# Attention products of blocks 2 to 8 as quarter-array matmuls

## The chip, the cores and the metric

The kernel runs on one core of a Trainium2 chip. The metric is the device time of one execution in microseconds (us), from the first to the last instruction of the core.

## What is computed

Attention within chunks of 64 tokens, for 8 batches, 8 heads, 576 tokens and a head width of 64; the 512 numbers that the heads leave for each of the 4608 tokens then go through a gated feed-forward layer of width 1536. All of it is float32.

```python
scores = scale * np.matmul(q_c, k_c.transpose(0, 1, 2, 4, 3))     # per chunk: 64 x 64 by 64
scores = scores - np.max(scores, axis=-1, keepdims=True)
attn = np.exp(scores)
attn = attn / (np.sum(attn, axis=-1, keepdims=True) + 1e-09)
out = np.matmul(attn, v_c)                                        # per chunk: 64 x 64 by 64
...
gate = 1.0 / (1.0 + np.exp(-(x @ w_gate)))
val = x @ w_val
return (gate * val @ w_out).astype(np.float32)
```

## The kernel before

**Blocks and units.** The tokens are worked through in 9 blocks of 512 (`m` = 0 to 8). The attention of a block is 4 units: `units[j]` is (block, half of the block's tokens, half of the heads), so block `m` has the units `4m` to `4m+3`. A unit holds 16 chunk products, laid out so that two heads lie on the two halves of the 128 partitions (`i`), and two others on the two halves of the result's partitions.

**Scores and values.** `products(j)` (lines 163 to 175) multiplies a unit's queries `qt` by its keys in 8 float32 matmuls. Each takes all 128 rows of TensorE's array and 64 of its 128 columns, and has 128 moving columns. Only 64 rows belong to one head, so the keys `kbd` are stored block-diagonally: head `i`'s keys on its own 64 partitions and zeros on the other 64, in a tile `[128, 2, 2, 256]` whose zeros are written once at the start. `values(j)` (lines 224 to 250) does the same with the softmax weights `pbd`, which are block-diagonal too, against the values `vt`: 8 matmuls of 64 by 128. Both write one PSUM bank per unit (`sc`, `av`, out of a pool of two banks with the tag `psa`). Consecutive matmuls alternate between the left and the right half of the array's columns (`c` in the scores, `a` in the values).

**How blocks 2 to 8 are interleaved.** The units from 8 on go in pairs through the generator `flow()` (lines 503 to 549). For a pair it issues, in this order: the score matmuls of both units (item "S"), the loads of the next pair, the last 4 of the 16 transposes of the pair before, maximum and subtraction on VectorE for each unit, one exponential on ScalarE, then the value matmuls of the pair before (item "A"), then sums, reciprocal, normalization, and 12 of the pair's own 16 transposes. `spread()` makes these on VectorE as 32 by 32 stream transposes out of `pr` into `pbd`. The items are pulled by `tick` and `insert` between steps of the feed-forward layer: the program order on TensorE and VectorE is the order in which this code runs, and is fixed when the kernel is built. There are 14 pairs (units 8 to 35), so 14 "S" bursts and 14 "A" bursts, each of 16 matmuls.

**The rest of TensorE's work.** For blocks 1 and 2, `hidden` and `down` make the feed-forward layer with matmuls in a split form (L261 and L287). Blocks 3 to 8 go in three pairs of blocks through a product scheme with 7 instead of 8 sub-products (`product`, L421) and the outward product (L496). These are 128 by 128 by 512 matmuls on `F32R` data, whose halves of higher and lower bits are made by ScalarE and VectorE.

**Evacuation.** From block 3 on, one ScalarE copy per unit (L242) moves `av` to a tile `raw`; in block 2 a ScalarE cast (L249) and a VectorE subtraction (L250) make the two `F32R` parts.

**Loads.** SP's queue issues all loads: `qt` by one transfer per unit, `kbd` by two (L152, one per half of the partitions, because the zeros lie between), `vt` by one.

Of the kernel before, what the change touches and what calls it, by code (L numbers as in the profile page):

```python
# [8 lines left out]
F32 = mybir.dt.float32  # L9
F32R = mybir.dt.float32r  # L10
U32 = mybir.dt.uint32
AF = mybir.ActivationFunctionType
ALU = mybir.AluOpType
AX = mybir.AxisListType

P = 128
D = 64
NB = 9
TB = 512
# [20 lines left out]
VECTOR_TRANSPOSES = 8  # L40

FIRST_PAIR = 3


SHARES = {1: 2.5, 2: 2.8, "up": 1.05, "down": 1.3}
# [3 lines left out]
def chunk_attn_moe(ctx: ExitStack, tc: tile.TileContext, q, k, v, w, out):  # L49


    nc = tc.nc
# [3 lines left out]
    xp = ctx.enter_context(tc.tile_pool(name="xp", bufs=4))  # L56
# [5 lines left out]
    ps_a = ctx.enter_context(tc.tile_pool(name="ps_a", bufs=2, space=bass.MemoryType.PSUM))  # L62
# [9 lines left out]
    pbd2 = const.tile([P, 2, 8, 2, D], F32, name="pbd")  # L72
# [67 lines left out]
    units = [(m, h, u) for m in range(NB) for h in range(2) for u in range(2)]  # L140
    state, both = {}, {}
    xt, raw = {}, {}

    def load(j):
        m, h, u = units[j]
        g = 2 * m + h
        qt = ap2.tile([P, 2, 256], F32, name="qt")
        kb = kbd[j % 2]
        nc.sync.dma_start(qt, q[g, u].rearrange("p (a n) -> p a n", a=2))
        for i in range(2):  # L150
            s = slice(i * D, (i + 1) * D)
            nc.sync.dma_start(kb[s, :, i, :], k[g, u, s].rearrange("p (a n) -> p a n", a=2))  # L152
        state[j] = dict(qt=qt, kb=kb)

    def load_values(j):
        m, h, u = units[j]
        vt = ap2.tile([P, 2, 4, D], F32, name="vt")
        nc.sync.dma_start(vt, v[2 * m + h, u].rearrange("p (a c d) -> p a c d", a=2, c=4))
        state[j]["vt"] = vt
# [3 lines left out]
    def products(j):  # L163
        s = state[j]
        sc = ps_a.tile([P, 512], F32, tag="psa", name="sc")
        for a in range(2):
            for t in range(2):
                for c in ((0, 1), (1, 0))[a * t]:
                    n0 = (2 * t + c) * D
                    nc.tensor.matmul(  # L170
                        sc[c * D:(c + 1) * D, (2 * a + t) * P:(2 * a + t + 1) * P],
                        lhsT=s["qt"][:, a, n0:n0 + D], rhs=s["kb"][:, a, :, n0:n0 + D],
                        start=True, stop=True,
                    )
        return sc.rearrange("p (g k) -> p g k", k=D)
# [48 lines left out]
    def values(j):  # L224
        m, h, u = units[j]
        s = state.pop(j)
        pb = pbd[j % 2]
        av = ps_a.tile([P, 512], F32, tag="psa", name="av")
        for c in range(4):
            for a in ((0, 1), (1, 0))[c == 3]:  # L230
                nc.tensor.matmul(  # L231
                    av[a * D:(a + 1) * D, c * P:(c + 1) * P],
                    lhsT=s["vt"][:, a, c, :], rhs=pb[:, 4 * a + c, :, :],
                    start=True, stop=True,
                )
        avv = av.rearrange("p (c h q) -> p h c q", h=2, q=D)
        if m >= FIRST_PAIR:
            n, half = divmod(m - FIRST_PAIR, 2)
            if (n, u) not in raw:
                raw[n, u] = xp.tile([P, 2, 2, TB], F32, tag="x", name="raw")  # L240
            dst = raw[n, u][:, :, half, h * 256:(h + 1) * 256]
            nc.scalar.copy(dst.rearrange("p h (c q) -> p h c q", q=D), avv)  # L242
            return
        if h == 0:
            xt[m, u] = xp.tile([P, 2, 2, TB], F32R, tag="x", name="xt")
        x = xt[m, u]
        hi = x[:, 0, :, h * 256:(h + 1) * 256].rearrange("p h (c q) -> p h c q", q=D)
        lo = x[:, 1, :, h * 256:(h + 1) * 256].rearrange("p h (c q) -> p h c q", q=D)
        nc.scalar.copy(hi, avv)  # L249
        nc.vector.tensor_tensor(out=lo, in0=avv, in1=hi.bitcast(F32), op=ALU.subtract)  # L250


    def up(m, f, which, tok):
# [40 lines left out]
    def evacuate(m, t, last=False):  # L294
        rows = out[m * TB + t * P:m * TB + (t + 1) * P, :]
        if last:
            ob = wp.tile([P, DM], F32, tag=f"u{t}", name="ob")
        elif m < FIRST_PAIR - 1 or t < 2:
            ob = mp.tile([P, DM], F32, name="ob")
# [91 lines left out]
    def operands(n):  # L391


        low = None
        for i, (name, (u, b), less) in enumerate(MADE):
            at = raw[n, u][:, :, b]
            if less:
                (u0, b0), (u1, b1) = less
                yield 1.2
                nc.vector.tensor_tensor(out=at, in0=raw[n, u0][:, :, b0], in1=raw[n, u1][:, :, b1], op=ALU.subtract)  # L400
            t = wp.tile([P, 2, 2, TB], F32R, tag=f"u{i}", name="xc")
            nc.scalar.copy(t[:, 0], at)
            if low:
                yield from lower(*low)
            low = n, name, t, at
        yield "wait"
        yield from lower(*low)
# [95 lines left out]
    def flow():  # L503


        kept = None
        for j in range(8, 4 * NB + 2, 2):
            more = j < 4 * NB
            if more:
                yield "S"  # L510
                scv = [products(j), products(j + 1)]
                if j + 2 < 4 * NB:
                    load(j + 2), load(j + 3)
                if kept:
                    yield from spread(*kept, range(12, 16))
                pr = ap2.tile([P, 2, 8, D], F32, name="pr", bufs=1)
                for i in range(2):
                    yield 1.4
                    mx = sm.tile([P, 8], F32, name="mx")
                    nc.vector.reduce_max(out=mx, in_=scv[i], axis=AX.X)  # L520
                    nc.vector.tensor_tensor(
                        out=pr[:, i], in0=scv[i], in1=mx.unsqueeze(2).broadcast_to([P, 8, D]), op=ALU.subtract)
                pr = pr.rearrange("p u g k -> p (u g) k")
                nc.scalar.activation(pr, pr, AF.Exp, scale=0.125)
            elif kept:
                yield from spread(*kept, range(12, 16))
            if kept:
                yield "A"
                values(j - 2), values(j - 1)
                if more:  # L530
                    load_values(j), load_values(j + 1)
            else:
                yield "wait"
            n, rest = divmod(j - 4 * FIRST_PAIR, 8)
            if n > 0 and rest == 0:
                yield ("open", n - 1)
                yield from operands(n - 1)
            if not more:
                return
            yield 1.5  # L540
            sums = sm.tile([P, 16], F32, name="sums2", bufs=1)
            nc.vector.reduce_sum(out=sums, in_=pr, axis=AX.X)
            nc.vector.tensor_scalar_add(out=sums, in0=sums, scalar1=1e-9)
            inv = sm.tile([P, 16], F32, name="inv2", bufs=1)
            nc.vector.reciprocal(out=inv, in_=sums)
            yield 1.2
            nc.vector.tensor_tensor(out=pr, in0=pr, in1=inv.unsqueeze(2).broadcast_to([P, 16, D]), op=ALU.mult)  # L547
            kept = pr, pbd2
            yield from spread(*kept, range(12))

    def spread(pr, pb, which):

        ps = pr.rearrange("p g (k j) -> p g k j", j=32)
        pb = pb.rearrange("p u (x c) h (i q) -> p (u x) c h i q", c=2, q=32)
        for n in which:
            c, i, h, k = n >> 3, n >> 2 & 1, n >> 1 & 1, n & 1
            src = slice((2 * c + i) * 32, (2 * c + i + 1) * 32)
            dst = slice((2 * h + k) * 32, (2 * h + k + 1) * 32)
            yield 0.44
            nc.vector.transpose(out=pb[dst, :, c, h, i, :], in_=ps[src, h::2, k, :])  # L560

    ahead = flow()
    now = dict(item=next(ahead), credit=0.0, ticks=0, since=0, unit=8, open=-1)

# [67 lines left out]
    kept = [(p, which, c) for p in range(6) for which in range(2) for c in range(2)]  # L632
# [9 lines left out]
    def rest():  # L642
        for m in range(1, FIRST_PAIR):
            upto = 4 * (m + 2) if m == 1 else 4 * (m + 3)
# [19 lines left out]
        for n in range(3):  # L664
            m0 = FIRST_PAIR + 2 * n
            upto = 4 * (m0 + 4)
# [77 lines left out]
```

## Time and profile before

| what | value |
|---|---|
| median of 3 runs | 955.29 us (955.13 to 955.56) |
| span of the profiled execution | 955.7 us (the profile shows nothing around it) |
| TensorE matmuls (PE) | 930.4 us, 97% of the span, 4960 records |
| VectorE (DVE) | 603.5 us, 63% |
| ScalarE (ACT) | 343.5 us, 36% |
| GpSimd (POOL) | 134.7 us, 14% |
| DMA, mean over 16 engines | 59.2% on the main queue |
| mean granted TensorE clock | 0.989 of full speed |

PE counts matmuls, PEld the loads of the stationary operand, which run beside matmuls. A busy share is time in which at least one instruction of the engine was under way. A float32 matmul of this kernel stands in the trace as two PE records and two PEld records (576 records each for the 288 score matmuls of 36 units); an `F32R` matmul as one of each. The "chain" is the work that ended last, followed back from the end of the span: what lies on it sets the time.

### The profile page before, as it was taken

The numbers are of one execution on the slowest core, as the hardware profiler recorded it, in microseconds if no ns is written. First come the engines' busy times: TensorE is split into PE (matmuls) and PEld (weight loads), VectorE is DVE, ScalarE is ACT, GpSimd is POOL, SyncE is SP. The second block draws the span as 40 slices with busy tenths as digits, with TensorE's granted clock in tenths as the row PEclk, the third lists the DMA queues.
The fourth block names the chain that finished last, engine by engine and source line by source line (L and its number), as shares of the span: only waits on it lengthen the run. The fifth ranks groups of instructions, "written<-read, shape, count | busy, mean of one in ns | idle before, by whom it ended". The sixth has DMA issues, their size and how long they took to land.

```text
span 955.7 us, 13079 instructions
## 1 busy us (share of the span) xinstructions
PE 930.4 (97%) x4960; PEld 764.1 (80%) x4960; DVE 603.5 (63%) x999; ACT 343.5 (36%) x558; POOL 134.7 (14%) x204
## 2 busy tenths in 40 slices
PE   5899999999999999999999999999999999999998
PEld 4777879888888887888887788888878888888886
DVE  5889875565676566867768575777586434545332
ACT  5889644232134343132242423213324321112222
POOL 1000004980049980000000000000000000000000
PEclk7899999999999999999999999999999999999999
DMA  8789886443233448666675756675555655556661
GB/s 262 215 292 306 285 293 198 133 133 88 67 123 121 133 149 292 198 210 200 213 238 218 242 199 213 208 230 200 197 198 205 206 206 188 198 187 209 220 220 45
DMA packets 81279, 189.61 MB, mean 198 GB/s; under 512 B 7488, under 2 KB 38208, under 8 KB 76608
## 3 DMA queue, kind: packets, MB, share of 16 engines
q1 hardware_dynamic: 81216, 188.77, 59.2%
q8 instruction: 39, 0.64, 0.3%
q14 instruction: 24, 0.20, 0.1%
HBM read 150.99 MB, written 37.75 MB: 197 GB/s over the span
## 4 chain that ended last, share of the span: by engine, by line
PE 88%; ACT 4%; DVE 4%; DMA 3%; issue 1%; SPq 0%; ACTq 0%; DVEq 0%
PE acc L496 20%; PE g L261 17%; PE cy L421 15%; PE cz L421 10%; PE cx L421 10%; PE acc L287 9%; PE sc L170 4%; PE av L231 3%; DMA w_raw<-w_in 2%; DMA kbd<-k_in 1%; ACT w_raw L129 1%; ACT w_raw L130 1%; ACT w L136 0%; DVE w L137 0%; ACT early L195 0%
## 5 line engine op out<-in xcount | busy, mean ns | idle before, releaser
L261 PE MATMUL g<-xt,w 128*128 128x512 f32 (+1 forms) x960 | 208.5, 372 | 9.5 <-ACT w L136 4.1
L261 PEld LDWEIGHTS g<-xt,w 128*128 128x128 f32 x960 | 168.4, 190 | 43.6 <-ACT w L136 4.3
L496 PE MATMUL acc<-wr,hh 128*128 128x512 f32 x576 | 177.8, 390 | 0.0
L421 PE MATMUL cy<-xc,wr 128*128 128x512 f32 x648 | 159.2, 389 | 0.9 <-DVE u L439 0.9
L421 PEld LDWEIGHTS cy<-xc,wr 128*128 128x128 f32 x648 | 121.5, 188 | 26.5 <-DVE u L439 1.3
L496 PEld LDWEIGHTS acc<-wr,hh 128*128 128x128 f32 x576 | 107.9, 188 | 22.7 <-ACT raw L242 0.3
L496 PE MATMUL acc<-wr,hl 128*128 128x512 f32 x288 | 112.7, 391 | 2.7 <-DVE hl L488 2.7
L421 PE MATMUL cz<-xc,wr 128*128 128x512 f32 x432 | 106.0, 391 | 0.0
L421 PE MATMUL cx<-xc,wr 128*128 128x512 f32 x432 | 106.0, 391 | 0.0
L560 DVE STREAM_TRANSPOSE pbd<-pr 32x256 f32<-32x256 f32 x224 | 97.7, 436 | 4.4 <-DVE pr L547 0.5
L488 DVE TENSOR_TENSOR hl<-hid,hh 128x512 fp32r<-128x512 f32 x72 | 49.4, 688 | 78.8 <-ACT hh L486 78.4
L421 PEld LDWEIGHTS cx<-xc,wr 128*128 128x128 f32 x432 | 80.6, 188 | 17.5 <-issue 1.0
L421 PEld LDWEIGHTS cz<-xc,wr 128*128 128x128 f32 x432 | 80.6, 188 | 17.5 <-issue 1.0
L287 PE MATMUL acc<-w,hh 128*128 128x512 f32 x288 | 91.3, 399 | 0.0
L486 ACT CAST hh<-hid 128x512 fp32r<-128x512 f32 x72 | 44.8, 622 | 127.1 <-PE acc L496 103.7
L496 PEld LDWEIGHTS acc<-wr,hl 128*128 128x128 f32 x288 | 54.0, 188 | 16.0 <-DVE hl L488 4.8
L338 POOL TENSOR_TENSOR a_val<-w 128x256 f32<-128x256 f32 x48 | 36.8, 787 | 211.6 <-DMA out<-ob 210.0
L439 DVE TENSOR_TENSOR u<-cy,s 128x512 f32<-128x512 f32 x36 | 24.8, 688 | 63.4 <-PE cy L421 63.1
L272 DVE TENSOR_TENSOR hf<-g,hf 128x512 f32<-128x512 f32 (+1 forms) x40 | 25.4, 635 | 60.9 <-PE g L261 60.3
L287 PEld LDWEIGHTS acc<-w,hh 128*128 128x128 f32 x288 | 53.2, 190 | 12.1 <-issue 1.9
L456 DVE TENSOR_TENSOR u<-cy,s 128x512 f32<-128x512 f32 x36 | 24.9, 691 | 50.9 <-PE cy L421 50.7
L287 PE MATMUL acc<-w,hl 128*128 128x512 f32 x144 | 56.5, 392 | 0.0
(103 smaller groups left out, 1013.8 us busy)
## 6 DMA issues: line engine op xcount, KB each, us to landing
wr<-sums SPq DMA_DIRECT2D x72, 512.0 KB, 4.6
wr<-outer SPq DMA_DIRECT2D x36, 1024.0 KB, 4.8
w_raw<-w_in SPq DMA_DIRECT2D x36, 512.0 KB, 5.3
wr<-given SPq DMA_DIRECT2D x36, 512.0 KB, 3.7
sums<-a_both SPq DMA_DIRECT2D x24, 512.0 KB, 3.5
qt<-q_in SPq DMA_DIRECT2D x36, 256.0 KB, 4.3
kbd<-k_in SPq DMA_DIRECT2D x72, 128.0 KB, 4.4
vt<-v_in SPq DMA_DIRECT2D x36, 256.0 KB, 3.9
```

The source lines that it names most:

```text
L170: nc.tensor.matmul(sc[c * D:(c + 1) * D, (2 * a + t) * P:(2 * a + t + 1) * P], lhsT=s["qt"][:, a, n0:n0 + D], rhs=s["kb"][:, a, :, n0:n0 + D],
L231: nc.tensor.matmul(av[a * D:(a + 1) * D, c * P:(c + 1) * P], lhsT=s["vt"][:, a, c, :], rhs=pb[:, 4 * a + c, :, :], start=True, stop=True,)
L261: nc.tensor.matmul(ps[:, tok], lhsT=wt[f, which][:, wpart, c:c + P], rhs=x[:, part, i, tok], start=n == 0, stop=n == 11)
L272: nc.vector.tensor_tensor(out=hf, in0=pv, in1=hf, op=ALU.mult)
L287: nc.tensor.matmul(acc[m, t], lhsT=hx[:, ts], rhs=wt[f, 2][:, wpart], start=f == 0 and i == 0, stop=f == NF - 1 and i == 2,)
L338: nc.gpsimd.tensor_tensor(out=val[:, 2 * n:2 * n + 2], in0=parts[:, 0], in1=parts[:, 1], op=ALU.add)
L421: nc.tensor.matmul(bank, lhsT=lhs(wpart, c), rhs=x[:, part, c], start=start and k == 0, stop=stop and k == 5, skip_group_check=True)
L456: nc.vector.tensor_tensor(out=u3, in0=y, in1=s1, op=ALU.add)
L486: nc.scalar.copy(hh, h)
L488: nc.vector.tensor_tensor(out=hl, in0=h, in1=hh.bitcast(F32), op=ALU.subtract)
L496: nc.tensor.matmul(acc[m, t], lhsT=hx[:, ts], rhs=wo[f][:, wpart], start=f == 0 and i == 0, stop=f == NF - 1 and i == 2)
L560: nc.vector.transpose(out=pb[dst, :, c, h, i, :], in_=ps[src, h::2, k, :])
```

## The change

From unit 8 on, the products no longer go through the whole height of the array. `tiled_products` makes the scores of a pair in 32 matmuls of 64 by 64 by 64: each takes 64 rows and 64 columns of the array, a quarter, and has 64 moving columns. The four quarters take turns in program order: column half `c` outside, row half `i` inside. The two row halves write to two PSUM banks, so that each bank now holds one row half of both units, where it held both row halves of one unit. `tiled_values` does the same for the values of a pair. Both still take two `psa` banks per pair.

With it go these edits. The keys are loaded by one transfer per unit into half of the `kbd` tile, without zeros. The transposes write the 64 by 64 blocks of `pbd` densely, into one half of that tile for each pair in turn, instead of block-diagonally into both halves. The evacuation is four ScalarE copies of 128 by 256 per pair instead of two of 128 by 512 (in block 2, four casts and four subtractions). Units 0 to 7 are as before. The first of several matmuls in a burst waits for its bank: the wait for the second bank now stands at the burst's second matmul, not at its ninth.

```diff
     def load(j):
...
+        if j >= FIRST_TILED:
+            kt = kb[:, :, 0, :]
+            nc.sync.dma_start(kt, k[g, u].rearrange("p (a n) -> p a n", a=2))
+            state[j] = dict(qt=qt, kt=kt)
+            return
         for i in range(2):
             s = slice(i * D, (i + 1) * D)
             nc.sync.dma_start(kb[s, :, i, :], k[g, u, s].rearrange("p (a n) -> p a n", a=2))
...
+    def tiled_products(j):
+        sc = [ps_a.tile([P, 512], F32, tag="psa", name="sc") for _ in range(2)]
+        for u in range(2):
+            s = state[j + u]
+            for a in range(2):
+                for t in range(2):
+                    n0 = ((2 * u + a) * 2 + t) * D
+                    for c in range(2):
+                        chunk = slice((2 * t + c) * D, (2 * t + c + 1) * D)
+                        for i in range(2):
+                            rows = slice(i * D, (i + 1) * D)
+                            nc.tensor.matmul(
+                                sc[i][c * D:(c + 1) * D, n0:n0 + D],
+                                lhsT=s["qt"][rows, a, chunk], rhs=s["kt"][rows, a, chunk], start=True, stop=True)
+        return [x.rearrange("p (g k) -> p g k", k=D) for x in sc]
+
+    def tiled_values(j, pt):
+        m, h, _ = units[j]
+        av = [ps_a.tile([P, 512], F32, tag="psa", name="av") for _ in range(2)]
+        vt = [state.pop(j + u)["vt"] for u in range(2)]
+        for u in range(2):
+            for c in range(4):
+                n0 = (4 * u + c) * D
+                for a in range(2):
+                    for i in range(2):
+                        rows = slice(i * D, (i + 1) * D)
+                        nc.tensor.matmul(
+                            av[i][a * D:(a + 1) * D, n0:n0 + D],
+                            lhsT=vt[u][rows, a, c, :], rhs=pt[rows, u, a, c, :], start=True, stop=True)
...
+            for i in range(2):
+                src = av[i][:, u * 256:(u + 1) * 256]
+                if m >= FIRST_PAIR:
+                    nc.scalar.copy(raw[n, u][:, i, half, cols], src)
+                else:
+                    hi, lo = (xt[m, u][:, part, i, cols] for part in range(2))
+                    nc.scalar.copy(hi, src)
+                    nc.vector.tensor_tensor(out=lo, in0=src, in1=hi.bitcast(F32), op=ALU.subtract)
...
-                scv = [products(j), products(j + 1)]
+                scv = tiled_products(j)
...
-                values(j - 2), values(j - 1)
+                tiled_values(j - 2, kept[1])
...
-            kept = pr, pbd2
+            kept = pr, pbd2[:, j // 2 % 2].rearrange("p (u a c) h q -> p u a (c h) q", u=2, a=2)
...
-        pb = pb.rearrange("p u (x c) h (i q) -> p (u x) c h i q", c=2, q=32)
+        pb = pb.rearrange("p u a (t c) (i q) -> p (u a t) c i q", c=2, q=32)
...
-            nc.vector.transpose(out=pb[dst, :, c, h, i, :], in_=ps[src, h::2, k, :])
+            nc.vector.transpose(out=pb[dst, :, c, i, :], in_=ps[src, 8 * h:8 * (h + 1), k, :])
```

TensorE's program order around the last "S" burst (units 34 and 35, in the pair of blocks 7 and 8), before the change. `cz` and `cy` are banks of the feed-forward products, `sc` the scores; what stands in brackets are the semaphores that an instruction waits for.

```order
L421 MATMUL cz<-xc,wr 128x512 [waits DVE_49]
L421 MATMUL cz<-xc,wr 128x512 x5
L170 MATMUL sc<-kbd_87,qt 64x128 [waits PE_49]
L170 MATMUL sc<-kbd_87,qt 64x128 x7
L170 MATMUL sc<-kbd_88,qt 64x128 [waits DMAHW4_49,PE_49]
L170 MATMUL sc<-kbd_88,qt 64x128 x7
L421 MATMUL cz<-xc,wr 128x512 x6
L421 MATMUL cy<-xc,wr 128x512 [waits DMAHW1_49,DVE_49]
```

The same place on TensorE after the change (line 475 is line 421 of before, line 271 is in `tiled_products`).

```order
L475 MATMUL cz<-xc,wr 128x512 [waits DVE_49]
L475 MATMUL cz<-xc,wr 128x512 x5
L271 MATMUL sc<-kbd_87,qt 64x64 [waits PE_49] x2
L271 MATMUL sc<-kbd_87,qt 64x64 x14
L271 MATMUL sc<-kbd_88,qt 64x64 [waits DMAHW0_49]
L271 MATMUL sc<-kbd_88,qt 64x64 x15
L475 MATMUL cz<-xc,wr 128x512 x6
L475 MATMUL cy<-xc,wr 128x512 [waits DMAHW5_49,DVE_49]
```

The burst stands between the same neighbours; 16 matmuls of 128 moving columns became 32 of 64.

TensorE's program order around the "A" burst that follows it, before the change (`av` are the attention's values, `cx` a bank of the feed-forward products).

```order
L421 MATMUL cx<-xc,wr 128x512 [waits Activation_49]
L421 MATMUL cx<-xc,wr 128x512 x5
L231 MATMUL av<-pbd,vt 64x128 [waits DMAHW4_49,DVE_49,PE_49]
L231 MATMUL av<-pbd,vt 64x128 x7
L231 MATMUL av<-pbd,vt 64x128 [waits DVE_49,PE_49]
L231 MATMUL av<-pbd,vt 64x128 x7
L421 MATMUL cx<-xc,wr 128x512 [waits DMAHW6_49]
```

The same place on TensorE after the change (line 286 is in `tiled_values`).

```order
L475 MATMUL cx<-xc,wr 128x512 [waits Activation_49]
L475 MATMUL cx<-xc,wr 128x512 x5
L286 MATMUL av<-pbd,vt 64x64 [waits DMAHW0_49,DVE_49,PE_49]
L286 MATMUL av<-pbd,vt 64x64 [waits DVE_49,PE_49]
L286 MATMUL av<-pbd,vt 64x64 x30
L475 MATMUL cx<-xc,wr 128x512 [waits DMAHW2_49]
```

The wait for VectorE to leave the second bank moved from the ninth matmul of the burst to the second; the neighbours are the same. On VectorE the order of instructions is unchanged.

More of the change, by code (lines that the diff above doesn't have):

```diff
@@ L42 @@
 FIRST_PAIR = 3
+FIRST_TILED = 8
 SHARES = {1: 2.5, 2: 2.8, "up": 1.05, "down": 1.3}
@@ L250, in values @@
         nc.vector.tensor_tensor(out=lo, in0=avv, in1=hi.bitcast(F32), op=ALU.subtract)
+    def tiled_products(j):
[26 more added lines that the diff above has]
+                            lhsT=vt[u][rows, a, c, :], rhs=pt[rows, u, a, c, :], start=True, stop=True)
+        cols = slice(h * 256, (h + 1) * 256)
+        for u in range(2):
+            if m >= FIRST_PAIR:
+                n, half = divmod(m - FIRST_PAIR, 2)
+                if (n, u) not in raw:
+                    raw[n, u] = xp.tile([P, 2, 2, TB], F32, tag="x", name="raw")
+            elif h == 0:
+                xt[m, u] = xp.tile([P, 2, 2, TB], F32R, tag="x", name="xt")
+            for i in range(2):
+                src = av[i][:, u * 256:(u + 1) * 256]
+                if m >= FIRST_PAIR:
+                    nc.scalar.copy(raw[n, u][:, i, half, cols], src)
[3 more added lines that the diff above has]
+                    nc.vector.tensor_tensor(out=lo, in0=src, in1=hi.bitcast(F32), op=ALU.subtract)
     def up(m, f, which, tok):
```

## The prediction

> **What bounds the kernel now.** I read the page first: the engines' shares, and the chain that ended last.
>
> ```profile
> PE 930.4 (97%) x4960; PEld 764.1 (80%) x4960; DVE 603.5 (63%) x999; ACT 343.5 (36%) x558; POOL 134.7 (14%) x204
> PE 88%; ACT 4%; DVE 4%; DMA 3%; issue 1%; SPq 0%; ACTq 0%; DVEq 0%
> PE acc L496 20%; PE g L261 17%; PE cy L421 15%; PE cz L421 10%; PE cx L421 10%; PE acc L287 9%; PE sc L170 4%; PE av L231 3%; DMA w_raw<-w_in 2%; DMA kbd<-k_in 1%; ACT w_raw L129 1%; ACT w_raw L130 1%; ACT w L136 0%; DVE w L137 0%; ACT early L195 0%
> ```
>
> The chain runs through TensorE for 88% of the span. The two lines of the attention products, L170 and L231, hold 4% and 3% of it. The next view is what TensorE waits for from 120 us on, where the changed bursts lie:
>
> ```profile
> PE acc L496 <- DVE hl L488: 2.7, 5, 1.0
> PE cy L421 <- DVE u L439: 0.9, 1, 0.9
> PE g L261 <- DVE hf L272: 0.7, 1, 0.7
> ```
>
> That is the whole list: 4.3 us of waiting in 836 us, none of it for a DMA. So time that TensorE no longer needs in a burst is time off the end, as long as no other engine falls behind. The chain of waits in order of time shows what a burst costs, here "S" of units 30 and 31 and the "A" that follows:
>
> ```profile
> 586.34 1.36 PE cz L421 x6
> 587.70 1.90 PE sc L170 x32
> 589.60 1.58 PE cz L421 x6
> 602.06 1.36 PE cx L421 x6
> 603.42 1.90 PE av L231 x32
> ```
>
> A burst holds 1.90 us of the chain, and the six matmuls behind it take 1.58 instead of 1.36: 2.12 us in all. How many bursts there are comes from the busy time of either line in the stretch where units 8 to 35 lie; L170 and L231 give the same row:
>
> ```profile
> 172.00:725.00 553.00, 27.55 (x448) 24.16 (x448) 1.00 0.56 184
> ```
>
> 448 records are 14 bursts of 32, for each line, so 28 bursts: 28 x 2.12 = 59.4 us of the span. The clock in that stretch is full (1.00).
>
> **The change: the matmuls.** How do 1.90 us come about? The timeline of TensorE in the burst at 672 us, cut off after more and more records, and then whole:
>
> ```profile
> 672.27 0.33 PE L170 MATMUL sc<-kbd,qt 128*64 128x128 f32 x2
> 672.27 0.44 PE L170 MATMUL sc<-kbd,qt 128*64 128x128 f32 x4
> 672.27 0.55 PE L170 MATMUL sc<-kbd,qt 128*64 128x128 f32 x6
> 672.27 1.97 PE L170 MATMUL sc<-kbd,qt 128*64 128x128 f32 x32
> ```
>
> Two records, one in each column half, start together, and every further two add 0.11 us: (1.97 - 0.33) / 15 = 0.109. The 16 slots are 1.75 us; the other 0.37 of the 2.12 are the entrance and exit (a first weight load, an emptied array, the slower matmul behind). A slot is spent on two things that overlap: 128 moving columns, and the weight load of the next record. The weight loads (PEld) of the same burst, 132 to 137 ns each:
>
> ```profile
> 672.27 0.14 PEld L170 LDWEIGHTS sc<-kbd,qt 128*64 128x64 f32 x2 [0.35 <-issue]
> 672.27 0.19 PEld L170 LDWEIGHTS sc<-kbd,qt 128*64 128x64 f32 x3 [0.35 <-issue]
> 672.27 0.20 PEld L170 LDWEIGHTS sc<-kbd,qt 128*64 128x64 f32 x4 [0.35 <-issue]
> ```
>
> Two loads, in two column halves, run at once, and the same half's next one starts about 0.05 us later. So a load of 64 columns occupies its part of the array for about 0.055 us, and that now sits hidden in 0.109.
>
> The change makes 32 products of 64 moving columns out of 16 of 128. If the four quarters run side by side, a slot holds four records instead of two, and there are again 16 slots: 64 records / 4. Half the columns bring a slot to 0.109 / 2 = 0.055, and the weight load just fits beneath: estimate 0.0555. 16 x 0.0555 = 0.89 us against 1.75: at best 0.86 us a burst, 28 x 0.86 = 24.1 us.
>
> The other bound is the rate at which products reach the array. It shows where the queue was empty, at the first scores of all, behind a wait for a DMA:
>
> ```profile
> 5.01 0.13 PEld L170 LDWEIGHTS sc<-kbd,qt 128*64 128x64 f32 x1 [1.33 <-issue]
> 5.01 0.17 PEld L170 LDWEIGHTS sc<-kbd,qt 128*64 128x64 f32 x2 [1.33 <-issue]
> ```
>
> The second product's first load, as long as the first's, ends 0.04 us later. At 672 us the two were at most 0.01 apart, because products stood ready while the matmuls before them ran. Were all 32 fed at 0.04, they would take 1.28 us, the gain would be 1.75 - 1.28 = 0.47 a burst and 13.2 us in all. I take a value near the first bound, since bursts start with a stock in hand and quarters need a product each 0.11 / 4 = 0.028 us, which outruns 0.04 only slowly: 0.06 above the best, so 0.80 a burst, **22.4 us**. Entrance and exit stay 0.37; if smaller matmuls emptied the array 0.05 sooner, that would be another 1.4 us.
>
> In this the records of a product must not hold up those of another quarter. A burst of three products, in program order right, right, left (units' lines 166 to 168, the last three), tells:
>
> ```profile
> 52.82 0.65 PE L170 MATMUL sc<-kbd,qt 128*64 128x128 f32 x6
> ```
>
> Started strictly in order, the left half's two records would begin with the fourth slot, five slots in all: 0.05 + 4 x 0.109 + 0.27 for the last = 0.76 us. It took 0.65, four slots, as if each half had its own line. The Trainium skill says otherwise (TensorE: Matmul & The Clock Gate, "Part 3: Packing small matmuls — row/col tiling"): matmuls start and end strictly in program order, only weight loads overtake. By that rule every product would add its own slot, 32 x 0.0555 = 1.78 us, and nothing would be gained; the row of 0.65 speaks against it for column halves.
>
> **Evacuation.** The nearest rows for copies half as wide, each behind the row of the form that goes:
>
> ```profile
> L242 ACT COPY raw<-av 128x512 f32<-128x512 f32 x24 | 13.4, 584 | 1.9 <-PE av L231 1.9
> L270 ACT ACTIVATE hf<-g 128x256 f32<-128x256 f32 x8 | 3.1, 382 | 3.6 <-PE g L261 3.0 <-DVE hl L276 0.6
> L249 ACT CAST xt<-av 128x512 fp32r<-128x512 f32 x12 | 6.8, 588 | 0.4 <-PE av L231 0.3
> L274 ACT CAST hh<-hf 128x256 fp32r<-128x256 f32 x8 | 3.3, 411 | 5.2 <-DVE hf L272 5.2
> L250 DVE TENSOR_TENSOR xt<-av,xt 128x512 fp32r<-128x512 f32 x12 | 7.9, 682 | 0.1
> L276 DVE TENSOR_TENSOR hl<-hf,hh 128x256 fp32r<-128x256 f32 x8 | 4.1, 518 | 3.5 <-ACT hh L274 3.5
> ```
>
> Per pair from block 3 on: 4 x 382 - 2 x 584 = +360 ns on ScalarE, 12 times; in block 2 4 x 411 - 2 x 588 = +468 ns there and 4 x 518 - 2 x 682 = +708 ns on VectorE, twice. Together 5.3 and 1.4 us on engines that are 36% and 63% busy. Behind an "A" burst in the outward phase ScalarE's next cast, and VectorE behind it, are late at times; TensorE already waits once there:
>
> ```profile
> 542.98 0.50 PE L496 MATMUL acc<-wr,hl 128*128 128x512 f32 x1 [0.25 <-DVE hl L488]
> ```
>
> Two "A" bursts lie so (537 and 722 us). I take 0.5 us; the ends are nothing and the whole 5.3.
>
> **Waits moved.** The "A" burst needs both banks left by VectorE at its start, not the second one half a burst later. In the tightest case of before:
>
> ```profile
> 592.58 0.69 DVE L456 TENSOR_TENSOR u<-cy,s 128x512 f32<-128x512 f32 x1 [4.15 <-PE cy L421]
> 602.27 0.69 DVE L521 TENSOR_TENSOR pr<-sc,mx 128x512 f32<-128x512 f32 x1
> 603.35 1.97 PE L231 MATMUL av<-pbd,vt 128*64 128x128 f32 x32
> ```
>
> The second subtraction ends at 602.96, 0.39 us ahead. Between the "S" burst and this place VectorE waited 4.15 us for TensorE, so it is timed anew behind the shortened burst and the 0.39 stay: cost nothing, and up to 0.4 a burst (5.6 us) if that cover went; the rest of the feed-forward matmuls would queue behind.
>
> **Loads and transposes.** One key transfer per unit goes:
>
> ```profile
> L152 SPq DMA_DIRECT2D kbd<-k_in x72: 533/594/1345, 1.2 to 634.8; - x72
> ```
>
> 28 x 0.594 = 16.6 us less on SP's queue, for which TensorE did not wait: nothing. The transposes keep their count and their 32 by 256 shape, only their steps differ: nothing; a tenth more each would be under 10 us on VectorE, beside TensorE.
>
> **Sum.** 955.7 - 22.4 + 0.5 = 933.8 us on the span; the median of the runs is 0.4 below it: **933.4 us**.
>
> **The rivals.** *Issue sets the pace* (chance 0.13). The array has quarters free, but products come at the 0.04 us of the empty queue: 955.3 - 13.2 + 0.5 = 942.6. For it: twice the instructions for the same arithmetic. Against it: the stock at each burst's start. The Trainium skill has a rule of this kind against the change (TensorEngine Tiling (Array Packing), "Instruction Overhead"): a matmul costs about 60 cycles however few columns it moves, so a factor shouldn't be taken out of a dimension that is already small. With the 2.4 GHz of its TensorE page, 64 records of 25 ns would be an estimated 1.6 us, a gain of 0.15 a burst and about 951 us. No row here shows such a floor; starts of two records 0.01 us apart show that it doesn't hold between column halves.
>
> *The row halves take turns* (0.09). No row of before has row halves, so that they run side by side isn't shown. If only one works in a column at a time, each column half does 32 records of 0.0555: 1.78 us, 28 x 0.03 = +0.8, and +0.5: 956.6, no change. The same 1.78 us comes out if products are started strictly in order, each quarter's second record holding up the next product (against it: the row of 0.65); both share this chance. The tiling page, "Key Properties", says that tiles load and multiply independently, which speaks against this.
>
> *Weight loads lie bare* (0.08, slower). The row halves take turns, and a half's load can't hide under the other's matmul: 32 x (0.055 + 0.0555) = 3.54 us, +1.79 a burst: 955.3 + 50.1 + 0.5 = 1006. It turns from gain to loss where TensorE starts a record less often than every 1.75 / 64 = 27 ns. Against it: PEld rows show loads of two halves at once, under running matmuls.
>
> **How the numbers follow.** The forecast has the remaining 0.70. Its own range is 930 (24.1 gained, 1.4 at the exits) to 939 (5.6 lost to the moved wait). The range of 8 in 10 runs from 929.5 to 951, and so takes in the pace rival with its whole span; the last two are left out. About 0.2% is what a measurement can tell here: faster by more 0.83 (forecast and pace), within it 0.09, slower 0.08.
>
> **What would show it.** Right: a burst has 64 records in about 1.0 us on the chain, the six matmuls behind it keep 1.58, and TensorE waits for nothing new. Pace: four records start, then gaps, with 1.3 us or more. Turns: 1.8 us, starts in twos. Bare loads: over 3 us. I am wrong in the second place if TensorE waits for VectorE at the start of "A", or for ScalarE's casts behind it.

## The result, and the profile after

| | median | ratio to before |
|---|---|---|
| before | 955.21 us (952.15 to 955.56, 4 runs) | |
| after | 942.51 us (941.23 to 945.38, 4 runs) | 0.9879, 95% interval 0.9857 to 0.9900 |

The kernel is 12.7 us faster, 9.1 us slower than forecast. The profiled execution of after took 945.38 us with a span of 943.6, so 1.8 us lie around the span, and it is the longest of the four; that of before had a span of 955.7, and the balance below goes from span to span.

The page of after, first the engines' shares and the chain:

```profile
PE 911.6 (97%) x5856; PEld 746.7 (79%) x5856; DVE 604.2 (64%) x1003; ACT 343.5 (36%) x586; POOL 141.7 (15%) x204
PE 73%; DMA 9%; POOL 7%; ACT 4%; DVE 4%; issue 1%; SPq 1%; POOLq 0%; DVEq 0%; ACTq 0%
PE acc L550 19%; PE cy L475 16%; PE cz L475 11%; PE cx L475 11%; PE g L315 9%; PE acc L341 5%; DMA w_raw<-w_in 4%; POOL a_sum L398 2%; POOL a_both L401 2%; POOL a_val L392 2%; DMA sums<-a_both 2%; PE sc L271 1%; PE av L286 1%; POOL a_both L400 1%; DMA wr<-sums 1%
```

TensorE held 88% of the chain and now holds 73%. GpSimd, absent before, has 7%, and DMA went from 3% to 9%. `a_val`, `a_sum` and `a_both` are lines of `keep_sums`, a function that the change doesn't touch. A chain that leaves the bounding engine says that somewhere this engine stood still. What TensorE waited for from 120 us on:

```profile
PE cz L475 <- DMA wr<-sums: 8.5, 1, 8.5
PE acc L550 <- DVE hl L542: 2.9, 5, 1.0
PE cy L475 <- DVE u L493: 0.9, 1, 0.9
PE g L315 <- DVE hf L326: 0.5, 1, 0.5
```

Three of the four rows are those of before. The first is new: one wait of 8.5 us, for a load. The bursts themselves did what was forecast. The chain in order of time, an "S" burst and what follows it, then an "A" burst:

```profile
171.80 1.09 PE sc L271 x64
172.89 1.59 PE acc L341 x6
...
409.85 1.09 PE av L286 x64
410.94 1.59 PE cz L475 x6
```

1.09 us where 1.90 stood, and the six matmuls behind still take 1.59. The gain is 0.81 us a burst. The busy time of either line between 170 and 715 us holds all of its 14 bursts, 16.26 us against 27.55, and (27.55 - 16.26) / 14 = 0.806:

```profile
170.00:715.00 545.00, 16.26 (x896) 14.34 (x896) 0.99 0.55 188
```

28 x 0.806 = 22.6 us gained. The timeline of TensorE in one burst, cut off later and later, shows the slot:

```profile
662.94 0.29 PE L271 MATMUL sc<-kbd,qt 64*64 64x64 f32 x4
662.94 0.34 PE L271 MATMUL sc<-kbd,qt 64*64 64x64 f32 x8
662.94 1.16 PE L271 MATMUL sc<-kbd,qt 64*64 64x64 f32 x64
```

Four records start together, and every further four add (1.16 - 0.34) / 14 = 0.0586 us: four quarters side by side, a slot 3 ns over the estimate.

Where did 10 of the 22.6 us go? The chain around the wait in order of time (start, length, what; "SPq" is SP's queue issuing a DMA):

```profile
354.69 1.35 POOL a_both L400
356.08 2.20 POOLq L794
358.30 0.52 SPq L402
358.87 0.63 SPq L154
...
361.22 0.59 SPq L422
361.91 0.38 SPq L419
362.33 7.76 DMA wr<-sums
370.23 2.90 PE cz L475 x6
```

Read upwards: TensorE's first product of block 3 (L475) waits for the load of sums and differences of weight blocks (L422; two loads, issued at 361.22 and 362.33, and the second is the one it waits for). They stand on SP's queue behind loads of keys and queries, and these behind the last store of such sums (L402), which waits until GpSimd has made them. The sums loaded here are those of the first pieces, which SP stored between 162 and 180 us; by this chain they wait for the last piece because SP works in order. Whether that alone holds them back is tried below. And GpSimd's time doesn't shrink with the bursts. Its last piece in the timeline of after, and TensorE's last matmul ahead of block 3:

```profile
356.12 2.15 POOL L401 TENSOR_TENSOR a_both<-a_sum,a_both 128x512 fp32r<-128x512 f32 x1
...
361.29 0.39 PE L341 MATMUL acc<-w,hl 128*128 128x512 f32 x1
```

The same in before, with SP's two loads of the sums (in after at 361.22 and 362.33) and TensorE's last matmul ahead of block 3 and its first one in block 3:

```profile
356.37 2.16 POOL L347 TENSOR_TENSOR a_both<-a_sum,a_both 128x512 fp32r<-128x512 f32 x1
362.06 0.59 SPq L368 DMA_DIRECT2D wr<-sums  x1
363.17 0.43 SPq L368 DMA_DIRECT2D wr<-sums  x1
...
372.86 0.39 PE L287 MATMUL acc<-w,hl 128*128 128x512 f32 x1
373.09 1.52 PE L421 MATMUL cz<-xc,wr 128*128 128x512 f32 x6
```

And how long the second load took to land, in before and in after:

```profile
L368 SPq DMA_DIRECT2D wr<-sums x1: 430/430/430, 363.2 to 363.2; - x1
DMA to landing us min/median/max: 6.6/6.6/6.6
```

```profile
L422 SPq DMA_DIRECT2D wr<-sums x1: 430/430/430, 362.3 to 362.3; - x1
DMA to landing us min/median/max: 7.8/7.8/7.8
```

GpSimd ended 0.3 us earlier after the change and the load was issued 0.84 us earlier, but TensorE came 11.6 us earlier: its last matmul ahead of this place starts at 361.29 instead of 372.86. It had saved 0.8 us in each of the 13 bursts that lie ahead of block 3, and its first changed burst had started 1.2 us earlier. In before the load was there at 363.17 + 6.6 = 369.8 us, 3.3 us ahead of TensorE. That was the cover. In after it landed at 370.1, 0.3 us later than before, since it took 1.2 us longer. So the wait is 11.6 - 3.3 + 0.3 = 8.6 us, and the list says 8.5.

There is a second price. The windows of after around the wait (stretch, length, busy PE, PEld, DVE, ACT, POOL, then granted clock, DMA share, GB/s):

```profile
361.00:370.00 9.00, 0.68 (x4) 0.22 (x2) 3.05 (x4) 1.13 (x2) 0.00 (x0) 0.79 0.98 324
370.00:376.50 6.50, 6.27 (x15) 5.01 (x16) 0.69 (x1) 0.58 (x1) 0.00 (x0) 0.51 1.02 400
376.50:400.00 23.50, 22.65 (x159) 18.28 (x158) 17.62 (x32) 4.53 (x7) 0.00 (x0) 1.00 0.58 196
```

For 6.5 us after the wait TensorE is busy at a granted clock of 0.51: about 3.1 us lost. The Trainium skill (TensorE: Matmul & The Clock Gate, "Part 1: The HAM clock gate") has the clock halve after at least one idle window of about 3.4 us and come back after at least one busy one. The trace agrees on the half; here the clock was back some 6 us after TensorE went on.

The balance of the spans: 955.7 - 22.6 (bursts) + 8.5 (wait) + 3.1 (clock) = 944.7, and 1.2 us by which the first changed burst started earlier (171.73 instead of 172.90) make 943.5, against 943.6. What made the 1.2 us isn't shown; between the profiled executions of all the kernels here the start of that burst varies from 168.0 to 172.9.

### The profile page after: what moved, and what is told of

The parts are those of the page before. It is cut to its first block, busy times and chain, and to the rows that moved or that the text cites. A ratio compares the mean times of both kernels' runs of the same rounds, so it can differ in the third digit from the quotient of the medians.

```text
span 943.6 us, 14868 instructions
## 1 busy us (share of the span) xinstructions
PE 911.6 (97%) x5856; PEld 746.7 (79%) x5856; DVE 604.2 (64%) x1003; ACT 343.5 (36%) x586; POOL 141.7 (15%) x204
## 4 chain that ended last, share of the span: by engine, by line
PE 73%; DMA 9%; POOL 7%; ACT 4%; DVE 4%; issue 1%; SPq 1%; POOLq 0%; DVEq 0%; ACTq 0%
PE acc L550 19%; PE cy L475 16%; PE cz L475 11%; PE cx L475 11%; PE g L315 9%; PE acc L341 5%; DMA w_raw<-w_in 4%; POOL a_sum L398 2%; POOL a_both L401 2%; POOL a_val L392 2%; DMA sums<-a_both 2%; PE sc L271 1%; PE av L286 1%; POOL a_both L400 1%; DMA wr<-sums 1%
## 5 line engine op out<-in xcount | busy, mean ns | idle before, releaser
L475 PE MATMUL cy<-xc,wr 128*128 128x512 f32 x648 | 159.2, 390 | 0.9 <-DVE u L493 0.9
L475 PEld LDWEIGHTS cy<-xc,wr 128*128 128x128 f32 x648 | 121.6, 188 | 26.5 <-DVE u L493 1.3
L550 PEld LDWEIGHTS acc<-wr,hh 128*128 128x128 f32 x576 | 107.9, 188 | 22.4
L475 PE MATMUL cz<-xc,wr 128*128 128x512 f32 x432 | 107.5, 395 | 8.5 <-DMA wr<-sums 8.5
L475 PE MATMUL cx<-xc,wr 128*128 128x512 f32 x432 | 106.1, 391 | 0.0
L475 PEld LDWEIGHTS cz<-xc,wr 128*128 128x128 f32 x432 | 81.4, 190 | 25.9 <-issue 8.9
L475 PEld LDWEIGHTS cx<-xc,wr 128*128 128x128 f32 x432 | 80.7, 188 | 16.9
L341 PEld LDWEIGHTS acc<-w,hh 128*128 128x128 f32 x288 | 54.0, 192 | 11.6 <-ACT xt L256 0.2
```

The source lines that it names most:

```text
L341: nc.tensor.matmul(acc[m, t], lhsT=hx[:, ts], rhs=wt[f, 2][:, wpart], start=f == 0 and i == 0, stop=f == NF - 1 and i == 2,)
L475: nc.tensor.matmul(bank, lhsT=lhs(wpart, c), rhs=x[:, part, c], start=start and k == 0, stop=stop and k == 5, skip_group_check=True)
L550: nc.tensor.matmul(acc[m, t], lhsT=hx[:, ts], rhs=wo[f][:, wpart], start=f == 0 and i == 0, stop=f == NF - 1 and i == 2)
```

## The experiments

**Theory A:** the bursts gain what was forecast, and the late sums take about half back, once, at the start of block 3. **The rival:** the loss is spread, the early bursts' gain or something that comes with every burst being worth less than the chain says; then it wouldn't matter which bursts are changed, and the wait would only be where it becomes visible.

**Sums made earlier.** In block 1 a second piece of the sums is made in every other step, so that fewer are left for block 2:

```diff
-                    keep(1)
+                    keep(1 + f % 2)
```

> The changed kernel, with GpSimd's sums begun earlier: in block 1 one or two of the 24 pieces per step in turn (15 pieces instead of 10), so 9 instead of 14 are left for block 2. Theory A (all 28 bursts give 0.81 us as their records show, and 11.7 us are lost in one place at the start of block 3: 8.5 us of waiting for sums that GpSimd finishes too late and that hold SP's queue, and about 3 us of a lowered clock behind the idle time): the wait and the low clock go, GpSimd ends before 340 us, time 932 +- 1.5. Theory B (the wait is for the loads themselves, since the DMA engines are 98% busy in that stretch, whatever GpSimd does): the wait stays within 2 us of 8.5 and the time at 941 to 943.

932.82 us (932.23 to 934.75), ratio 0.9765 (0.9747 to 0.9784) to a before of 954.31 on the same chip. What TensorE waits for from 120 us on, the last piece of GpSimd, and the chain at the start of block 3:

```profile
PE acc L550 <- DVE hl L542: 2.9, 5, 1.0
PE cy L475 <- DVE u L493: 0.9, 1, 0.9
PE sc L271 <- DMA kbd<-k_in: 0.4, 1, 0.4
```

```profile
322.31 1.29 POOL L401 TENSOR_TENSOR a_both<-a_sum,a_both 128x512 fp32r<-128x512 f32 x1
```

```profile
358.75 2.72 PE acc L341 x12
361.47 1.36 PE cz L475 x6
362.83 2.72 PE acc L341 x12
```

GpSimd ends at 323.6 instead of 358.3, the wait for the sums is gone, and so is the slow clock: `cz` x6 takes 1.36 instead of 2.90. As theory A has it. This is the fastest version found.

**The same edit on the kernel before.** Is it worth something by itself?

```diff
-                    keep(1)
+                    keep(1 + f % 2)
```

> The kernel before with the same earlier sums as in e1. Theory A: before the change TensorE came to block 3 late enough, nothing waited there, so nothing changes: 955.2 +- 1.5. If the earlier sums are worth something by themselves (a rival for e1's gain: less pressure on DMA or on shared ports), it shows here as a gain of some us as well.

953.73 us (952.45 to 955.12), ratio 0.9989 (0.9978 to 0.9999). At most 0.2%. So earlier sums bring little where TensorE comes late, and much where it comes early: the gain over the before of the same series grows from 12.7 to 21.5 us. With the sums out of the way on both sides the change is worth 953.73 - 932.82 = 20.9 us; the interval of the two ratios leaves about 2 us to either side, and the forecast's 21.9 lies in it.

**Late bursts only, early bursts only.** The quarter products are used from unit 22 on, or only up to unit 21 (with the zeros that the block-diagonal form needs put back at unit 22); seven pairs each.

```diff
+def tiled(j):
+    return j >= 22
...
-        if j >= FIRST_TILED:
+        if tiled(j):
...
-                scv = tiled_products(j)
+                scv = tiled_products(j) if tiled(j) else [products(j), products(j + 1)]
```

> Quarters only for units 22 to 35, the old products for units 8 to 21: 14 of the 28 bursts are changed, all of them behind the start of block 3. Theory A: TensorE reaches block 3 as late as before, there is no wait for sums, and 14 x 0.81 = 11.3 us are gained: 944 +- 1.5. Rival (every burst is worth the measured 12.7 / 28 = 0.45 us, the loss is spread): 949.

> The mirror of e3: quarters for units 8 to 21, the old products from unit 22 on, with six small fills of zeros on VectorE at the switch (about 3 us there, beside TensorE). Theory A: 14 bursts give 11.3 us, which are lost again at the start of block 3 (about 11.7 us of waiting and low clock): 955.5 +- 2, no change, with the 8 us wait for sums in the trace. Rival (loss spread over all bursts): 949.

Late only: 943.11 us (942.33 to 944.17), ratio 0.9872 (0.9854 to 0.9889), no wait for the sums. Early only: 952.73 us (948.66 to 956.81), ratio 0.9978 (0.9959 to 0.9997), and the wait is there, here in the profiled execution, the fastest of its twelve:

```profile
PE cz L481 <- DMA wr<-sums: 5.3, 1, 5.3
```

GpSimd ended at 352.6 us in this execution, earlier than the 358.3 of after, which fits the shorter wait; the slower executions left no profile.

To the before of 954.31, 14 late bursts gain 11.2 us, 0.80 each, the forecast's figure. The 14 early ones, 13 of them ahead of the start of block 3, gain 1.6. The two add up to 12.8, the whole change's 12.7. The late bursts lose nothing, so the loss isn't spread: the rival is out. Most of what the early bursts save is lost at the start of block 3.

**Which way does GpSimd's lateness reach TensorE?** First the stores of the sums are issued by GpSimd instead of SP, so that SP's queue no longer waits for them:

```diff
-        nc.sync.dma_start(
+        nc.gpsimd.dma_start(
             sums[p, which][:, :, c], both.rearrange("p s a n -> p s (a n)").bitcast(F32))
```

> The changed kernel, with the 24 stores of GpSimd's sums issued from GpSimd's own queue instead of SP's. The load that TensorE waits for reads the first sums, which were made 190 us earlier; it only stands in SP's queue behind the store of the last ones. Theory A1 (SP's queue in order is what makes TensorE wait): the wait of 8.5 us goes although GpSimd ends as late as before (about 358 us), 933 +- 2. Theory A2 (GpSimd's work itself is late: its last result is what is needed): the wait stays, 941 to 943. If stores from GpSimd's queue slow its own work, it ends later than 358 us, which A1 allows without loss.

951.73 us (946.91 to 954.0), ratio 0.9960 (0.9933 to 0.9987): neither forecast. What TensorE waits for from 120 us on:

```profile
PE cy L475 <- DVE u L493: 3.9, 1, 3.9
PE cx L475 <- DVE ob L361: 3.8, 1, 3.8
PE acc L550 <- DVE hl L542: 2.9, 5, 1.0
PE cy L475 <- ACT ob L359: 1.0, 1, 1.0
```

This is the fastest of the six executions; the slower ones left no profile. The wait for the sums is gone, and 7.8 us of others stand in its place (8.7 in three rows, of which 0.9 was there before). GpSimd was busy 159.1 us instead of 141.7 and made its last piece at 374.6; the output copies of block 2 (L359, L361) use buffers of the tag `ob`, which `a_val` and `a_sum` use too, and ScalarE's copy waited 10.5 us for GpSimd. SP still waited 11.7 us for a piece of GpSimd's (`a_val`), whose weights lie in the buffers that the load is to fill. So SP's order isn't the only way.

Then the stores stay on SP, and the first group's loads go to ScalarE's queue, two steps later in the code:

```diff
-            nc.sync.dma_start(
+            queue.dma_start(
...
-                    if f == 8:
-                        for which in range(2):
-                            load_group(0, 0, which)
+                    if f == 10:
+                        load_group(0, 0, 0, nc.scalar)
+                        load_group(0, 0, 1)
```

> The changed kernel, with its late sums as they are, but the four loads of the first group (weights and sums for block 3's first product) issued on ScalarE's queue instead of SP's, two steps later in the code. Theory A1 (the load of the first sums is late only because it stands on SP behind stores that wait for GpSimd): ScalarE issues it as soon as GpSimd has read the weights whose buffers it takes, about 348 us instead of 361, it lands about 9 us later, before TensorE needs it at 361.5; no wait for the sums, 933 +-2 us. Theory A2 (the weights that GpSimd still reads, or the buffers it shares, hold it back by themselves): the load starts no sooner and TensorE waits about as in the changed kernel, 941 to 944. Between them, 936 to 940, if ScalarE's casts, queued behind the loads, make TensorE wait in another place.

946.11 us (945.58 to 948.08), ratio 0.9932 (0.9906 to 0.9957) to 953.18: again neither. ScalarE's timeline, and TensorE's:

```profile
327.73 0.60 ACT L324 ACTIVATE hf<-g 128x512 f32<-128x512 f32 x1 [5.35 <-PE g L315]
347.37 0.34 ACTq L419 DMA_DIRECT2D wr<-given  x1
347.76 0.62 ACT L328 CAST hh<-hf 128x512 fp32r<-128x512 f32 x1 [19.43 <-DMA sums<-a_both]
349.30 0.33 ACTq L422 DMA_DIRECT2D wr<-sums  x1
```

```profile
351.37 1.98 PE L286 MATMUL av<-pbd,vt 64*64 64x64 f32 x62 [12.54 <-DVE pr L575]
```

Off SP's queue the two loads of the first sums start at 349.3 and 356.9 instead of 361.2 and 362.3, and TensorE doesn't wait for them at block 3. But ScalarE's first load too had to wait, until 347.3, when one of the last stores of sums had landed, and ScalarE's cast was queued behind it. VectorE waited for the cast, and TensorE for VectorE, 12.5 us. GpSimd itself ended earlier here, at 349.3, while VectorE stood still, so how much of the 12 and 5 us by which the loads came earlier is due to SP's order isn't told apart and stays open. What the two runs show is that GpSimd's lateness has several ways to TensorE, and that an edit on one of them uncovered the next. Only making the sums earlier, at the source, removed it.

**What sets the slot of 58 ns?** Both on top of the version with the earlier sums (932.82 us). First each product is split into two matmuls of 32 moving columns, again in turn over the quarters (scores here, values alike):

```diff
-                                lhsT=s["qt"][rows, a, chunk], rhs=s["kt"][rows, a, chunk], start=True, stop=True)
+                    for b in range(2):
...
+                                b0 = (2 * t + c) * D + 32 * b
...
+                                lhsT=s["qt"][rows, a, chunk], rhs=s["kt"][rows, a, b0:b0 + 32], start=True, stop=True)
```

> e1 with each 64 by 64 by 64 product as two matmuls of 32 moving columns, the quarters still in turn: the same results, twice the weight loads, the same columns moved. In the changed kernel a slot of four records takes 58 ns, where 64 columns at the pace of before take 55 and the weight load was read as 55. If a slot lasts as long as the weight load of the next record, it stays at 58 with 32 columns, 32 slots make a burst 0.93 us longer: 932.8 + 26 = 959. If the moving columns set it, a slot falls to about 30 and the time stays at 933. If products are fed at 0.04 us each, 64 of them take 2.6 us a burst: 978.

958.95 us (957.39 to 961.85), ratio 1.0044 (1.0014 to 1.0073). The burst in TensorE's timeline:

```profile
170.20 2.07 PE L273 MATMUL sc<-kbd,qt 64*64 64x32 f32 x128
```

Half the columns, twice the records, and the 16 slots added take 2.07 - 1.16 = 0.91 us, 57 ns each: a slot as long as with 64 columns. So it isn't the moving columns that fill it. A feed of one record every 15 ns would give the same slot in both kernels, but the single records in the trace rule it out: in the changed kernel's burst at 662.94 the four records of a slot start within 20 ns, and then none for 38 ns. What is left is what a record needs in its own quarter: the weight load, as the prediction read from the PEld rows ("about 0.055 us"), or another fixed cost of a record, which no run here tells apart from it.

Then the order is changed, all eight products of a quarter, then the next quarter (values alike):

```diff
-                    for c in range(2):
+        for c, i in ((0, 0), (0, 1), (1, 0), (1, 1)):
+            rows = slice(i * D, (i + 1) * D)
+            for u in range(2):
...
-                        for i in range(2):
-                            rows = slice(i * D, (i + 1) * D)
```

> e1 with the order of the products in a burst changed: all 8 of one quarter of the array, then all 8 of the next. If each quarter has its own line and about 7 products (28 records) stand ready ahead, as the trace suggests, two quarters overlap on the average: 16 products of 0.116 us in a row, 1.86 us a burst, 932.8 + 26 = 959. If far more stand ready, nothing changes: 933. If matmuls start strictly in order, nothing overlaps, 32 x 0.116 = 3.7 us a burst: 1010.

994.94 us (993.46 to 995.72), ratio 1.0415 (1.0387 to 1.0444): slower than before, and between two of the forecasts.

```profile
168.57 3.40 PE L270 MATMUL sc<-kbd,qt 64*64 64x64 f32 x64
```

Without any overlap the last record would start 63 slots of 0.0585 us after the first, at 3.69. A record is 0.22 us long, so it started at 3.40 - 0.22 = 3.18, some nine slots sooner, three at each of the three changes of quarter. The single records in the trace show the same: at the first change, three of the next quarter (169.33, 169.43 and 169.49 us) start before the last of the old quarter does, at 169.50. So TensorE does overtake, but here only some three records ahead, far fewer than the 28 that the expectation took to stand ready. The turn of the quarters in program order, four records in four quarters, is what the gain rests on.

## Why the prediction was right, and where it was wrong

**The burst: right.** Forecast 0.80 us each from a slot of 0.0555 and 0.06 for an imperfect feed; measured 0.806, from a slot of 0.0586 and a feed that holds it up no further. 22.6 us for 22.4. Entrance and exit kept their 1.59 us.

**Evacuation, transposes, the moved wait: right, and small.** Four ScalarE copies of 385 ns (forecast 382), transposes of 436 ns as before, TensorE's waits for VectorE in the outward phase 2.9 us in place of 2.7, where 0.5 more was set aside. At the tightest "A" burst the subtraction ended at 596.04 and the burst began at 596.42, 0.38 us apart (forecast 0.39).

**The step that failed** is the first one: "So time that TensorE no longer needs in a burst is time off the end, as long as no other engine falls behind", and in the sum, "for which TensorE did not wait: nothing". The list of waits was read as if no wait meant room without end. It shows which cover has run out, not how much is left of the others. GpSimd stands in the prediction with its 14% and in no term of the sum. But in before it works almost without a pause from 275 to 358.5 us, and loads that TensorE needs at 373 stand behind its last piece. Before an engine on the chain is made 11 us faster ahead of such a place, the transfers that it needs there have to be asked for their spare: issue 363.17, 6.6 us to land, 3.3 us spare. The step cost 8.5 us of waiting and 3.1 us of low clock in the profiled execution. Between the medians with late and with early sums it is 9.7 us, or 8.8 when each is set against the before of its own series: that is the miss of 9.1.

**Luck.** By its own sign ("TensorE waits for nothing new") the forecast failed. Its own range was 930 to 939 us; the 942.5 lies in the range of 8 in 10 only because that range also took in the pace rival, which is refuted below.

**The sum's base** was off as well: "the median of the runs is 0.4 below" compared a span with a time. Where a run of after shows both, they lie 1.8 us apart, so before's profiled execution was some 2 us above its median, and the two errors cancelled. With the earlier sums the kernel came to 932.8, the forecast less 0.6.

**The rivals.** *Issue sets the pace* gave 942.6, the number that was measured, and is refuted: its sign was to be a burst of 1.3 us or more, and it is 1.09, with four records started within 20 ns. That the value fits is chance. *The row halves take turns* and *weight loads lie bare* are refuted by the slot of four records in 0.0586 us. The Trainium skill's rule that matmuls start strictly in order (TensorE: Matmul & The Clock Gate, "Part 3") doesn't hold here for quarters in turn, but the quarter order shows that there is something in it: the overtaking goes about three records far, and beyond that program order holds. **The wait that was to prove it wrong** was expected at VectorE and ScalarE; it came by way of GpSimd's late work, in the changed kernel through SP's queue.

## What to carry to other kernels

Before making the bounding engine faster, look at every place where it meets work that others do in their own time, and work out how early each of its loads lands: the list of waits names only those that are already late. If the spare there is smaller than what is saved up to that place, the rest of the saving isn't had until the producer starts earlier; moving a store or a load to another queue only moved the wait here. Small products in the quarters of the array paid here because consecutive instructions go to different quarters, down to a slot of 58 ns for four records.

## What the runs showed of the hardware

- A slot of four float32 records in the four 64 by 64 quarters lasts 58 ns, with 64 moving columns or with 32. The likely floor is the weight load.
- Matmuls of another quarter overtake only about three records: 64 records took 1.16 us in turn and 3.40 us quarter after quarter.
- One wait of 8.5 us cost 3.1 us more behind it, at a granted clock of 0.51 for some 6 us. In the run with early bursts only, after a wait of 5.3 us, six `cz` matmuls took 2.90 us instead of 1.52, and from 367 us on, 3 us after TensorE went on, matmuls had their old length.
- GpSimd and VectorE hold each other up in some pairs of operations, not whenever both are busy. The windows of two stretches of after, each with one `a_both` subtraction on GpSimd (columns as above):

```profile
356.10:358.30 2.20, 2.20 (x11) 1.85 (x10) 2.20 (x2) 1.09 (x2) 2.15 (x1) 1.00 0.10 34
329.04:330.33 1.29, 1.29 (x8) 1.06 (x7) 1.23 (x4) 0.00 (x0) 1.29 (x1) 1.00 0.00 0
```

In the first stretch VectorE worked on the 128x1024 tiles `raw` and `xc`, and the subtraction took 2.15 us. In the second VectorE was almost as busy, with transposes and a maximum, and it took 1.29. VectorE's own `xc` subtraction took 2.31 us when it started within the first stretch, and 1.22 at 354.35, although GpSimd was busy for 0.89 us of that:

```profile
354.35 1.22 DVE L465 TENSOR_TENSOR xc<-raw,xc 128x1024 fp32r<-128x1024 f32 x1
...
357.04 2.31 DVE L465 TENSOR_TENSOR xc<-raw,xc 128x1024 fp32r<-128x1024 f32 x1
```

Each time the one that started second was the longer: GpSimd's at 356.12, 1.0 us ahead of the end of VectorE's `raw` operation (357.12), and VectorE's at 357.04, 1.2 us ahead of the end of GpSimd's (358.27). It looks as if they take turns in such a pair; no run tests it.
